# One core, one chain of attention, gated product and soft expert mixture: three moves in the schedule around the first block products

## The chip, the cores and the metric

The kernel runs as one program on one core of a Trainium2 chip. The core has five engines that run beside each other, each through its own list of instructions in order: TensorE (PE in the profile, with its weight loads as PEld), VectorE (DVE), ScalarE (ACT), GpSimd (POOL) and SyncE (SP, which here only issues DMAs). An engine that meets an instruction whose input is not there waits, and all that stands behind it in its list waits too. The metric is the device time of one execution in microseconds; lower is better.

## The reference, cut to what matters

```python
scores = scale * np.matmul(q, k.transpose(0, 1, 3, 2)) - np.log(S)   # 4 batches, 12 heads, S = 448, D = 64
attn = 1.0 / (1.0 + np.exp(-scores))
x = np.matmul(attn, v)            # then as (1792, 768)
x = (x @ w_a) * (x @ w_b) @ w_out # 768 -> 1536 -> 768
logits = x @ phi                  # 32 slots, softmax over tokens and over slots
d = softmax over tokens;  slot_input = d.T @ x
slot_out[e] = maximum(slot_input[e] @ w1[e], 0) @ w2[e]   # 8 experts, 4 slots each
return softmax over slots(logits) @ slot_out
```

## The kernel before

Attention runs in 24 pairs of heads, six for each of the four batches. A pair g needs its K and Q turned and split in two parts whose sum is the float32 value: `split_heads` writes kh, kl, qh and ql. From pair 13 on the turning is done by DVE (`transposed`, line 205), so that a pair costs DVE six instructions, in this order: transpose of K (kn), cast to kh (line 197), subtraction kl (line 198), transpose of Q (qn; a few pairs keep their Q in the tiles gk or hp, and rows name those), cast to qh, subtraction ql. In the dense stretch TensorE then does the scores of a pair in three chunks of two heads and three products each (line 260; the first chunk goes to a bank ms, and its third product is the one that reads ql), the part of the scores that two pairs share (line 275), and the product with V (line 294, and line 301 for the shared part). The sigmoids (line 266) are ACT's. ACT also copies a little of K (kr, line 228) for line 275. The result of a pair is copied from its bank by ACT or, for odd pairs, by DVE (line 323). These results, twelve tiles for batches 1 and 2, are the operands of what follows.

The products x @ w_a and x @ w_b of batches 1 and 2 are done together as one 2 by 2 block product in seven block products (Strassen's scheme with Winograd's additions), in twelve units of weight blocks; `unit` holds TensorE's side (line 874). Each of the seven has an operand made of x (A11, S2, A12, S3, S1, A22, S4) and one made of the weights. All are split in a high and a low part.

- `operands` makes the first three operands of x: casts on ACT or DVE, subtractions on POOL. For i in 0, 1, 2 it makes s2 by three subtractions on POOL (lines 800 to 802), and three steps later the cast S2h on DVE (line 782), the low part S2l on POOL (line 783), and a12 - s2 on POOL (line 806), which S4 needs later.
- `load_u(0)` has SP load 768 KB of weights (w_a and w_b as two fields) to the tile hp, line 737. `prep_u(0)` makes the second operands of the first unit from them: a cast on DVE (`block`, line 754) and a subtraction on POOL (line 755) for each of seven blocks, and four subtractions on POOL (lines 768 and 770) between the first block and the others. For all later units the cast is ACT's and the four subtractions are DVE's.

The order of all this is that of the program: a loop takes one step of attention (`att_g`), then one step of `operands`, and, in steps in which `operands` answers 0 or 1, one step of `prep_u`. SP issues DMAs in the same order; the loads of K, Q and V for pair g + 3 stand between those for the first unit. "Pair 16" and so on below are the values of g; results exist (`in xt`) as soon as their copy has been written down.

Behind the block products come the products of batch 3, done whole, and then the experts, whose weights (50 MB) are loaded in the order in which places for them come free, and the output tiles.

Of the kernel before, what the change touches and what calls it, by code (L numbers as in the profile page):

```python
# [14 lines left out]
ALU = mybir.AluOpType  # L15
# [12 lines left out]
NP = H // 2  # L28
# [3 lines left out]
GQ = 2 * NP + 2  # L32
# [9 lines left out]
def body(ctx, tc, q, k, v, w_a, w_b, w_out, phi, w1, w2, out):  # L42
    nc = tc.nc
    pe, act, dve, pool, sp = nc.tensor, nc.scalar, nc.vector, nc.gpsimd, nc.sync
# [11 lines left out]
    pools, r_all, hps_t = {}, [], []  # L56
# [27 lines left out]
    def gk_tile(i, dt=F32):  # L84
        return lgp.tile([128, 2048], dt, tag=f"lgp{i}", name=f"gk_{i}")

    gk_01 = [gk_tile(i) for i in range(2)]
# [216 lines left out]
    xt = {}  # L304
# [108 lines left out]
    late = []  # L413
# [175 lines left out]
    def fill_step():  # L589
        while fill:  # L590
            if next(fill[0], 0) is None:
                return
            fill.pop(0)
# [69 lines left out]
    def reload_gk(b, gi, t):  # L663
        if b in TURNED:
            sp.dma_start(out=t[:T], in_=gk32[b][gi].rearrange("t n f -> (t n f)").rearrange("(p x) -> p x", p=T))
            gtok[b, gi] = t.rearrange("p (c n) -> p c n", c=C)
            return
        t = t.rearrange("p (c n) -> p c n", c=C)
        src = gk32[b][gi].rearrange("n t f -> (n t) f")
        sp.dma_start(out=t[:, :3], in_=src[:384].rearrange("(c p) n -> p c n", c=3))  # L670
        sp.dma_start(out=t[64:, 3], in_=src[384:])
        gtok[b, gi] = t
# [59 lines left out]
    def load_u(u):  # L732
        if u > NU + 1:
            return
        t = hps_t[u % 2][:, :1536]
        src = ab32[u // 2 * 2:u // 2 * 2 + 2, u % 2] if u < NU else ab32[u - NU]
        sp.dma_start(out=t.rearrange("p (n c) -> p n c", n=2), in_=src.rearrange("n p c -> p n c"))
        if u < NU:
            wu[u] = t
        else:  # L740
            for i in range(2):
                w_raw[LAST + 2 * (u - NU) + i] = t[:, i * 768:(i + 1) * 768]
# [15 lines left out]
    def prep_u(u):  # L758

        w = wu.pop(u)  # L760
        b11, b21, b12, b22 = (w[:, i * BLK:(i + 1) * BLK] for i in range(4))
        t2, t3, t4 = (pools["cp"].tile([128, BLK], F32, tag=nm, name=nm) for nm in ("T2", "T3", "T4"))
        block(u, 0, b11)
        eng = dve if u else pool
        for o, a, b in ((t3, b22, b12), (b12, b12, b11), (t2, b22, b12)):
            if not u:
                yield
            eng.tensor_tensor(o, a, b, op=ALU.subtract)
        if not u:
            eng.tensor_tensor(t4, b21, t2, op=ALU.subtract)  # L770
            for _ in range(8):
                yield
        yield
        for m, t in ((1, t2), (2, b21), (3, t3), (4, b12), (5, t4), (6, b22)):
            if u and m == 5:
                eng.tensor_tensor(t4, b21, t2, op=ALU.subtract)  # L776
            block(u, m, t)
            yield

    def split_x(nm, i, t, pl, names, rnd=None, sub=None):  # L780
        xh, xl = (pl.tile([128, S], F32R, tag=x, name=x) for x in names)
        (rnd or dve.tensor_copy)(xh, t)
        (sub or pool).tensor_tensor(xl, t, xh.bitcast(F32), op=ALU.subtract)
        xs[nm, i] = xh, xl

    def operands():

        cp = pools["cp"]
        for i in range(3):
            split_x("A11", i, xt[NP + i], cp, (f"A11h{i}", f"A11l{i}"), act.copy)  # L790
            yield
            split_x("A12", i, xt[NP + 3 + i], cp, (f"A12h{i}", f"A12l{i}"), act.copy)
            yield
        for i in range(3):
            while 2 * NP + 3 + i not in xt:
                yield 1
            yield
            a11, a12, a21, a22 = (xt[n + i] for n in (NP, NP + 3, 2 * NP, 2 * NP + 3))
            s2 = cp.tile([128, S], F32, tag="s2", name="s2", bufs=2)
            pool.tensor_tensor(a11, a11, a21, op=ALU.subtract)  # L800
            pool.tensor_tensor(a21, a21, a22, op=ALU.add)
            pool.tensor_tensor(s2, a22, a11, op=ALU.subtract)
            for _ in range(3):
                yield
            split_x("S2", i, s2, cp, (f"S2h{i}", f"S2l{i}"))
            pool.tensor_tensor(a12, a12, s2, op=ALU.subtract)
            yield

    def late_operands(nm):
        n = {"S3": NP, "S1": 2 * NP, "A22": 2 * NP + 3, "S4": NP + 3}[nm]  # L810
# [388 lines left out]
    for kk in range(NP):  # L1199
# [6 lines left out]
    pools["cp"] = cp_ctx.enter_context(tc.tile_pool(name="cp", bufs=1, side="left"))  # L1206
    run["lsd2"] = (hps_t[0][:, 1536:1536 + S], hps_t[1][:, 1536:1536 + S], hps_t[2][:, 4 * S:4 * S + 128], hps_t[2][:, 4 * S + 128:])
    ops, pu = operands(), None
    then = [(2 * NP + 1, lambda: load_u(0)), (GQ + 5, lambda: reload_gk(0, 1, gk_01[1])),
            (GQ + 6, lambda: load_u(1)), (GQ + 7, lambda: reload_gk(0, 0, gk_01[0])),  # L1210
            (GQ + 7, lambda: reload_gk(0, 2, gk_2))]
    for cost in att_g:
        if then and then[0][0] in xt:
            then.pop(0)[1]()
        if not run.pop("trans", False):
            fill_step()
        run.pop("done", None)
        if next(ops, 0) in ((0, 1) if GQ + 1 in xt else (0,)):
            pu = pu or prep_u(0)
            next(pu, None)  # L1220
        if (4 * NP - 1, 0, C - 1) in a_t:
            break
# [97 lines left out]
    for n in range(0, len(order1), 4):  # L1320
        _, g, x, _ = order1[n]
# [7 lines left out]
        for j in range(4):  # L1329
            if order1[n + j] == order1[-1]:  # L1330
                _, pl, nm = ring.pop(order1[-1])
# [113 lines left out]
```

## Time and profile before

| | |
|---|---|
| median of three runs | 658.71 us (655.99, 658.71, 660.24) |
| the profiled execution's own time | 657.27 us |
| its span from the first to the last instruction | 655.5 us |
| TensorE, share of the span with a matmul in it | 96% |
| VectorE, ScalarE, GpSimd | 58%, 46%, 47% |
| attention in pairs 15 to 23, where the change lies | about 219 to 275 us |
| block products in twelve units | about 275 to 440 us |

Shares of the whole span say little here: the change lies in some 50 us of it, and there the engines' shares are others. Times in the rows below are microseconds from the first instruction. In the rows of the timeline the idle time in front of an instruction, and what ended it, stands at the end in brackets.

### The profile page before, as it was taken

Reading aid. Unit: us, or ns where it says so; the run is one execution under the profiler, and the core shown is the slowest. Engines: PE = TensorE matmul, PEld = TensorE weight load, DVE = VectorE, ACT = ScalarE, POOL = GpSimd, SP = SyncE. Lnnn points to the kernel's source line nnn. Section 1 sums busy time; section 2 is a strip of 40 time slices with the busy share of each in tenths; the row PEclk is TensorE's granted clock in tenths of the full one; section 3 lists DMA queues with packets and bytes.
Section 4 is the critical chain, followed back from the end, with each engine's and each line's share of the span. In section 5 each row is a group of like instructions: output and inputs, shape, how many; then the busy total and the mean of one; then the engine's idle time right before and its main releaser. Section 6 shows DMA issues by size and latency. Waiting matters only on the chain.

```text
span 655.5 us, 10847 instructions
## 1 busy us (share of the span) xinstructions
PE 627.6 (96%) x3989; PEld 448.3 (68%) x3989; DVE 379.5 (58%) x556; ACT 298.7 (46%) x540; POOL 309.5 (47%) x235
## 2 busy tenths in 40 slices
PE   8999999999999999999999999999999999996685
PEld 5556777777776554489988989897889895441121
DVE  4764877889793779488777766856233323030013
ACT  4988889889875877754422322201010002110012
POOL 0234587677772267369985576543335441000000
PEclk9999999999999999999999999999999999999788
DMA  9999889799778786901314332299899999999998
GB/s 222 265 284 259 262 281 342 248 298 298 255 178 209 138 165 118 287 2 48 97 50 104 91 109 75 81 241 307 239 359 405 414 340 366 419 399 416 409 369 298
DMA packets 148564, 159.76 MB, mean 244 GB/s; under 512 B 73584, under 2 KB 126640, under 8 KB 144432
## 3 DMA queue, kind: packets, MB, share of 16 engines
q1 hardware_dynamic: 145984, 157.35, 77.2%
q10 hardware_dynamic: 2528, 1.72, 0.8%
q8 instruction: 32, 0.52, 0.3%
q14 instruction: 20, 0.16, 0.1%
HBM read 129.11 MB, written 29.93 MB: 243 GB/s over the span
## 4 chain that ended last, share of the span: by engine, by line
PE 73%; DMA 14%; ACT 6%; DVE 3%; SPq 1%; issue 1%; POOL 1%; ACTq 0%; POOLq 0%; DVEq 0%
PE ab L686 22%; PE sc L874 16%; PE ab L874 8%; PE sc L260 6%; PE sc L288 4%; DMA misc<-clog 3%; PE ab L294 3%; DMA eb<-in_moe_w 2%; DMA e<-in_moe_w 2%; DMA hp<-in_moe_w 2%; ACT a L266 2%; DMA ea<-in_moe_w 1%; PE ms L600 1%; DMA ab<-w 1%; PE ms L213 1%
## 5 line engine op out<-in xcount | busy, mean ns | idle before, releaser
L472 POOL TENSOR_TENSOR w<-gk,cy 128x768 int32<-128x768 int32 x36 | 66.3, 1842 | 71.2 <-DVE gk L460 38.7
L266 ACT ACTIVATE a<-sc,sums 112x448 f32<-112x448 f32 (+1 forms) x149 | 84.0, 649 | 12.7 <-PE sc L260 12.7
L686 PE MATMUL ab<-t,wh 128*128 128x448 f32 x288 | 64.6, 370 | 0.0
L693 ACT COPY misc<-ab 128x448 f32<-128x448 f32 x24 | 12.7, 527 | 100.2 <-PE ab L686 100.2
L686 PEld LDWEIGHTS ab<-t,wh 128*128 128x128 f32 x288 | 53.7, 188 | 6.3 <-issue 1.3
L570 POOL TENSOR_TENSOR wl<-w,wh 128x768 fp32r<-128x768 f32 x24 | 46.1, 1923 | 11.5 <-ACT wh L569 11.5
L570 POOL TENSOR_TENSOR wl<-hp,wh 128x768 fp32r<-128x768 f32 x16 | 29.4, 1839 | 39.9 <-DVE wh L569 21.7
L288 PE MATMUL sc<-a,vn 112*64 112x448 f32 x192 | 38.7, 545 | 0.2 <-ACT a L266 0.2
L458 DVE TENSOR_SCALAR mf<-gk 128x768 f32<-128x768 f32 x24 | 22.7, 944 | 24.2 <-ACT gk L441 24.2
L696 DVE TENSOR_TENSOR misc<-misc,ab 128x448 f32<-128x448 f32 x24 | 14.7, 611 | 36.0 <-PE ab L686 36.0
L686 PE MATMUL ab<-xh,wl 128*128 128x448 f32 x144 | 34.8, 377 | 0.0
L754 ACT CAST wx<-T 128x384 fp32r<-128x384 f32 x19 | 9.7, 512 | 54.5 <-DVE T L776 36.7
L686 PE MATMUL ab<-xh,wh 128*128 128x448 f32 x144 | 34.5, 375 | 0.0
L686 PE MATMUL ab<-t,wl 128*128 128x448 f32 x144 | 34.3, 373 | 0.0
L686 PE MATMUL ab<-xl,wh 128*128 128x448 f32 x144 | 34.0, 372 | 0.0
L1404 DVE COPY o<-sc 128x384 f32<-128x384 f32 x10 | 5.4, 553 | 48.9 <-PE sc L1382 47.8
L755 POOL TENSOR_TENSOR wx<-hp,wx 128x384 fp32r<-128x384 f32 x27 | 31.5, 1171 | 4.6 <-DVE wx L754 2.5
L260 PE MATMUL sc<-qh,kh 64*112 64x448 f32 (+1 forms) x139 | 32.2, 432 | 1.0 <-ACT qh L197 0.6
L686 PEld LDWEIGHTS ab<-xh,wh 128*128 128x128 f32 x144 | 26.0, 188 | 7.3 <-issue 4.8
L686 PEld LDWEIGHTS ab<-xl,wh 128*128 128x128 f32 x144 | 26.4, 188 | 5.5 <-issue 3.5
L686 PEld LDWEIGHTS ab<-t,wl 128*128 128x128 f32 x144 | 26.6, 188 | 5.2 <-issue 2.0
L686 PEld LDWEIGHTS ab<-xh,wl 128*128 128x128 f32 x144 | 25.7, 188 | 5.1 <-issue 1.7
(509 smaller groups left out, 1571.3 us busy)
## 6 DMA issues: line engine op xcount, KB each, us to landing
hp<-ab SPq DMA_DIRECT2D x14, 768.0 KB, 4.4
gk<-gk SPq DMA_DIRECT2D x44, 224.0 KB, 4.3
ab<-w SPq DMA_DIRECT2D x24, 384.0 KB, 6.8
eb<-in_moe_w SPq DMA_DIRECT2D x7, 1024.0 KB, 12.8
ea<-in_moe_w SPq DMA_DIRECT2D x7, 1024.0 KB, 12.2
eb<-in_moe_w SPq DMA_DIRECT2D x7, 768.0 KB, 15.1
ea<-in_moe_w SPq DMA_DIRECT2D x7, 768.0 KB, 15.0
wr_cv<-in_moe_w_a SPq DMA_DIRECT2D x6, 768.0 KB, 8.0
```

The source lines that it names most:

```text
L260: pe.matmul(sc[h], kx[r, cs], qx[r], start=(i == 0), stop=(i == 2))
L266: act.activation(a, sc, AF.Sigmoid, bias=nlog[:n], scale=1.0 / math.sqrt(D))
L288: pe.matmul(pv[64 * h:64 * h + 64], qkv_t["v", g][:, h, c, :], a_t.pop((g, h, c)), start=(c == 0), stop=(c == C - 1))
L294: pe.matmul(pv[64 * h:64 * h + 64], qkv_t["v", g][:, h, c], a_t.pop((g, h, c)), start=(c == 0), stop=False)
L458: dve.tensor_scalar(mf, m, LOW, HIGH, op0=ALU.max, op1=ALU.min)
L472: pool.tensor_tensor(thirds(w), m.bitcast(I32), thirds(cy_t.pop(x)), op=ALU.add)
L570: pool.tensor_tensor(wl, t, wh.bitcast(F32), op=ALU.subtract)
L686: pe.matmul(t, w[:, kk * 128:(kk + 1) * 128], xt[b * NP + kk][xi], start=(s == 0 and kk == 0), stop=(s == 2 and kk == KD - 1))
L693: act.copy(gT_all[n % 5], t)
L696: dve.tensor_tensor(g, g, t, op=ALU.mult)
L755: pool.tensor_tensor(w[:, 1], t, w[:, 0].bitcast(F32), op=ALU.subtract)
L874: pe.matmul(t, w[:, wi, k * 128:(k + 1) * 128], xs[ORDER[m], k][xi], start=(s == 0 and k == 0), stop=(s == 2 and k == 2))
```

## The change

Three things change. (1) The cast S2h is written five steps behind its subtractions instead of three, and of the three subtractions a12 - s2 the second and the third are written behind all others. (2) `load_u(0)` is written when the result of pair 12 exists instead of pair 13's. (3) `prep_u(0)` may take steps from when pair 13's result exists, instead of pair 15's, in the steps in which `operands` waits for a result (it answers 1) as well as in those in which it has nothing left.

```diff
     def operands():
-        cp = pools["cp"]
+        cp, late = pools["cp"], []
...
-            for _ in range(3):
+            for _ in range(5):
                 yield
             split_x("S2", i, s2, cp, (f"S2h{i}", f"S2l{i}"))
+            if not i:
+                pool.tensor_tensor(a12, a12, s2, op=ALU.subtract)
+            else:
+                late.append((a12, s2))
+            yield
+        for a12, s2 in late:
             pool.tensor_tensor(a12, a12, s2, op=ALU.subtract)
-            yield
...
-    then = [(2 * NP + 1, lambda: load_u(0)), (GQ + 5, lambda: reload_gk(0, 1, gk_01[1])),
+    then = [(2 * NP, lambda: load_u(0)), (GQ + 5, lambda: reload_gk(0, 1, gk_01[1])),
...
-        if next(ops, 0) in ((0, 1) if GQ + 1 in xt else (0,)):
+        if next(ops, 0) in ((0, 1) if 2 * NP + 1 in xt else (0,)):
             pu = pu or prep_u(0)
             next(pu, None)
```

TensorE's and ScalarE's lists stay as they are. The list of SP around the weights' load (hp<-ab), before:

```order
L172 DMA vn<-in_v 128x2x192
L173 DMA vn<-in_v 64x2x64
L661 DMA gk_02_104<-gk_94 448x1x128 x4
L163 DMA kn<-in_k 32x14x32 x4
L163 DMA qn<-in_q 32x14x32 x4
L989 DMA clog_101<-hp_2474 448x1x32
L172 DMA gk_93<-in_v 128x2x192
L173 DMA gk_93<-in_v 64x2x64
L172 DMA gk_93<-in_v 128x2x192
L173 DMA gk_93<-in_v 64x2x64
L737 DMA hp_2472<-ab_99 128x2x768
L163 DMA kn<-in_k 32x14x32 x4
```

The same stretch of SP's list now:

```order
L172 DMA vn<-in_v 128x2x192
L173 DMA vn<-in_v 64x2x64
L737 DMA hp_2472<-ab_99 128x2x768
L661 DMA gk_02_104<-gk_94 448x1x128 x4
L163 DMA kn<-in_k 32x14x32 x4
L163 DMA qn<-in_q 32x14x32 x4
L994 DMA clog_101<-hp_2474 448x1x32
L172 DMA gk_93<-in_v 128x2x192
L173 DMA gk_93<-in_v 64x2x64
L172 DMA gk_93<-in_v 128x2x192
L173 DMA gk_93<-in_v 64x2x64
L163 DMA kn<-in_k 32x14x32 x4
```

The load has moved in front of 17 DMAs: four stores of gk, the K and Q of pair 18, one of clog and four for V. It now stands behind them no more, and the K of pair 19 follows V directly.

DVE's list, as one piece of the difference: the first two rows are the end of pair 15, the last three the beginning of pair 16, and between them stands the first cast of a block of weights, which before stood behind pair 18.

```order
 L197 CAST qh<-qn 128x448
 L198 TENSOR_TENSOR ql<-qn,qh 128x448
+L754 CAST wl_2698<-hp_2472 128x384
 L205 STREAM_TRANSPOSE kn<-kn 128x448
 L197 CAST kh<-kn 128x448
```

The next three casts of blocks move on the same list from behind pair 22 to behind pair 19 and the last three from behind pair 23 to behind pair 22. The cast S2h of i = 2, before in front of the copy of pair 19's result, is now behind it.

POOL's list from the last subtraction of A12 on, before:

```order
L783 TENSOR_TENSOR A12l_2594<-t_2398,A12h_2593 128x448
L800 TENSOR_TENSOR t_964<-t_964,hp_2474 128x448
L801 TENSOR_TENSOR hp_2474<-hp_2474,misc 128x448
L802 TENSOR_TENSOR s_2857<-misc,t_964 128x448
L783 TENSOR_TENSOR S2l_2909<-s_2857,S2h_2908 128x448
L806 TENSOR_TENSOR t_1791<-t_1791,s_2857 128x448
L755 TENSOR_TENSOR wl_2923<-hp_2472,wl_2923 128x384
L768 TENSOR_TENSOR T_2921<-hp_2472 128x384
L768 TENSOR_TENSOR hp_2472<-hp_2472 128x384
L768 TENSOR_TENSOR T_2920<-hp_2472 128x384
L770 TENSOR_TENSOR T_2922<-hp_2472,T_2920 128x384
```

POOL's list from there on now:

```order
L783 TENSOR_TENSOR A12l_2595<-t_2398,A12h_2594 128x448
L755 TENSOR_TENSOR wl_2698<-hp_2472,wl_2698 128x384
L768 TENSOR_TENSOR T_2696<-hp_2472 128x384
L768 TENSOR_TENSOR hp_2472<-hp_2472 128x384
L768 TENSOR_TENSOR T_2695<-hp_2472 128x384
L770 TENSOR_TENSOR T_2697<-hp_2472,T_2695 128x384
L800 TENSOR_TENSOR t_964<-t_964,hp_2474 128x448
L801 TENSOR_TENSOR hp_2474<-hp_2474,misc 128x448
L802 TENSOR_TENSOR s_2867<-misc,t_964 128x448
L783 TENSOR_TENSOR S2l_2938<-s_2867,S2h_2937 128x448
L807 TENSOR_TENSOR t_1791<-t_1791,s_2867 128x448
```

The five subtractions for the weights have changed places with the five for i = 0 of s2. Behind them come three more for the weights, then four for i = 1 and four for i = 2, then the two late ones and the last three for the weights.

## Rows read from the trace of the kernel before

**Rows 1.** The page's first part, busy time: engine, us (share), instructions.

```profile
PE 627.6 (96%) x3989; PEld 448.3 (68%) x3989; DVE 379.5 (58%) x556; ACT 298.7 (46%) x540; POOL 309.5 (47%) x235
```

**Rows 2.** Timeline of TensorE, 200 to 285 us: start, length, instruction, idle before it.

```profile
225.86 0.37 PE L260 MATMUL ms<-ql,kh 64*128 64x448 f32 x2
...
229.80 0.98 PE L301 MATMUL ab<-a,vn 64*64 64x448 f32 x8
...
232.82 2.48 PE L294 MATMUL ab<-a,gk 128*64 128x448 f32 x12
...
238.49 2.48 PE L294 MATMUL ab<-a,gk 128*64 128x448 f32 x12
...
244.42 2.48 PE L294 MATMUL ab<-a,vn 128*64 128x448 f32 x12
...
249.01 0.54 PE L260 MATMUL ms<-qh,kh 64*128 64x448 f32 x2 [0.62 <-DVE qh L197]
...
250.95 2.48 PE L294 MATMUL ab<-a,vn 128*64 128x448 f32 x12
...
256.38 2.48 PE L294 MATMUL ab<-a,gk 128*64 128x448 f32 x12
...
261.32 0.54 PE L260 MATMUL ms<-qh,kh 64*128 64x448 f32 x2 [0.97 <-DVE qh L197]
...
263.26 2.48 PE L294 MATMUL ab<-a,gk 128*64 128x448 f32 x12
265.91 1.50 PE L301 MATMUL ab<-a,gk 64*64 64x448 f32 x8 [0.17 <-ACT a L266]
```

**Rows 3.** Timeline of VectorE, pairs 16 and 19, a cast S2h, a cast of weights.

```profile
219.74 0.64 DVE L205 STREAM_TRANSPOSE kn<-kn 128x448 f32<-128x448 f32 x1
221.16 0.39 DVE L197 CAST kh<-kn 128x448 fp32r<-128x448 f32 x1 [0.78 <-PE sc L260]
...
223.23 0.62 DVE L198 TENSOR_TENSOR ql<-gk,qh 128x448 fp32r<-128x448 f32 x1
...
238.15 0.65 DVE L205 STREAM_TRANSPOSE kn<-kn 128x448 f32<-128x448 f32 x1 [1.38 <-DMA kn<-in_k]
238.90 1.19 DVE L197 CAST kh<-kn 128x448 fp32r<-128x448 f32 x1
...
242.58 1.32 DVE L198 TENSOR_TENSOR ql<-hp,qh 128x448 fp32r<-128x448 f32 x1
...
256.56 0.39 DVE L782 CAST S2h<-s 128x448 fp32r<-128x448 f32 x1 [1.06 <-POOL s L802]
...
262.02 0.35 DVE L754 CAST wl<-hp 128x384 fp32r<-128x384 f32 x1
262.29 1.16 DVE L754 CAST wx<-T 128x384 fp32r<-128x384 f32 x1
```

**Rows 4.** Timeline of GpSimd, the wait for pair 15's result and the weights' subtractions.

```profile
231.67 1.15 POOL L801 TENSOR_TENSOR hp<-hp,misc 128x448 f32<-128x448 f32 x1 [14.40 <-DVE misc L323]
...
238.84 1.00 POOL L755 TENSOR_TENSOR wl<-hp,wl 128x384 fp32r<-128x384 f32 x1
...
243.50 1.27 POOL L770 TENSOR_TENSOR T<-hp,T 128x384 f32<-128x384 f32 x1
```

**Rows 5.** Timeline of SyncE's DMA issues, 200 to 232 us.

```profile
217.97 0.65 SPq L173 DMA_DIRECT2D vn<-in_v  x1
...
231.17 0.59 SPq L737 DMA_DIRECT2D hp<-ab  x1
```

**Rows 6.** DMA issues at 231, at 263 and in 285 to 330 us: count, size, us to landing.

```profile
hp<-ab SPq DMA_DIRECT2D x1, 768.0 KB, 5.2
...
hp<-ab SPq DMA_DIRECT2D x1, 768.0 KB, 7.7
...
hp<-ab SPq DMA_DIRECT2D x3, 768.0 KB, 4.3
```

**Rows 7.** Busy time in stretches of the tail: PE, PEld, DVE, ACT, POOL, granted clock, DMA.

```profile
590.00:600.00 10.00, 5.94 (x50) 1.59 (x42) 0.00 (x0) 0.00 (x0) 0.00 (x0) 1.00 1.02 416
600.00:605.00 5.00, 3.61 (x30) 1.06 (x30) 0.00 (x0) 0.00 (x0) 0.00 (x0) 1.00 1.02 417
605.00:610.00 5.00, 3.52 (x18) 0.93 (x22) 0.00 (x0) 0.00 (x0) 0.00 (x0) 0.61 1.02 419
```

## The prediction

> **What bounds the kernel now.** I read the page's busy times first: TensorE has a matmul in 96% of the span [rows 1], so the most that any schedule can give is a few per cent, and the change can only touch what TensorE loses in the 50 us where instructions move. Next the timeline of TensorE there, for gaps and for rhythm. Gaps: 0.62 us at 249.0 and 0.97 us at 261.3, both ended by VectorE's qh, and 0.17 us at 265.9, ended by a sigmoid [rows 2]. Rhythm: the products with V begin at 232.82, 238.49, 244.42, 250.95, 256.38 and 263.26 [rows 2]. Undisturbed steps are 5.67 us (to 238.49, a step with the shared scores) and 5.43 us (250.95 to 256.38); the others are 5.93, 6.53 and 6.88, that is 0.50, 0.86 and 1.21 us too long. So 2.57 us are lost there, and with the 0.17 us about 2.7. That is all that a better order of VectorE's and GpSimd's work can win.
>
> Why VectorE is late is in its own timeline. Pair 16 has GpSimd idle beside it: from the start of its kn (219.74) to the end of ql (223.23 + 0.62 = 223.85) are 4.11 us, less a wait of 0.78, so 3.33 us of work; its cast kh takes 0.39 [rows 3]. Pair 19 has the block's subtraction and the four others beside it (238.84 to 243.50 + 1.27) [rows 4]: from 238.15 to the end of ql (242.58 + 1.32 = 243.90) are 5.75 us, with the cast kh at 1.19 and ql at 1.32 instead of 0.62 [rows 3]. So 4.4 GpSimd instructions cost VectorE 2.4 us, 0.55 each. A pair of TensorE lasts 5.5 us, so VectorE keeps up while GpSimd rests and falls behind while it works; and GpSimd rests 14.4 us in front of 231.67 [rows 4], where VectorE has room.
>
> The Trainium skill, "SBUF — State Buffer", section "Who interferes with whom", says why: casts in the fast mode and subtractions of two SBUF operands need a port that VectorE and GpSimd take in turn, each for a whole instruction. Taken strictly (four such instructions in a pair, each held back by a whole GpSimd instruction of about 1.15 us), pair 16 would take 3.33 + 4.6 = 7.9 us and the first stall below would be 2.2 us longer; the trace has 5.75 us for that case, so the sum goes by the trace.
>
> **The change part by part.** *The load goes sooner.* SP's issues follow each other closely, so the load is issued when the V load in front of it is out: 217.97 + 0.65 = 218.6, instead of 231.17 [rows 5]. A load of this size landed 5.2 us after issue at 231, 7.7 at 263 behind other large transfers, 4.3 in the quiet stretch [rows 6]. So it lands at 222.9 to 226.3; I take 5.2, the nearest in place and traffic, so 223.8. The loads that it delays by its own issue (0.6 us) are for pair 18, far ahead of their use. And it no longer stands in front of pair 19's K: VectorE's wait of 1.38 us for that at 238.15 [rows 3] should go.
>
> *The first cast goes sooner, too soon.* VectorE reaches it behind pair 15, when pair 16's kn starts now, at 219.74 [rows 3]. The data come at 223.8. VectorE waits about 4.1 us, and behind it in its list stand all six instructions of pair 16. TensorE needs the last of them, ql, at 225.86 [rows 2] and has it at 223.85, so 2.0 us of the wait are covered. After it come the cast, 0.35 alone [rows 3], and pair 16, now with GpSimd's five subtractions beside it as pair 19 has them today: 223.8 + 0.35 + 5.75 = 229.9. TensorE would be 4.0 us late there. Bounds: landing at 222.9 and 3.33 us for an undisturbed pair give 226.6, 0.7 us late; landing at 226.3 and 5.75 give 232.4, 6.5 us late. I take 4.0, since both its inputs are the nearest rows.
>
> *What comes back.* (a) Pair 17 on VectorE has one or two GpSimd instructions beside it, 3.33 + 0.8, and ends at 234.0; the copy of pair 15's result waits for line 301, which ends at 229.80 + 0.98 + 4.0 = 234.8 [rows 2]. So from here VectorE and TensorE are both 4.0 us behind the old trace. (b) In front of pair 19 VectorE loses neither the 1.38 us for K nor the first cast (0.35): 2.3 behind. Pair 19 has two GpSimd instructions beside it (S2l, and the first a12 - s2) instead of 4.4: 1.3 less, so 1.0 behind at its end. (c) Now three casts of weights stand here, 0.27 between the starts of two of them and 1.16 for the one beside GpSimd [rows 3], 1.7 together: 2.7 behind; their three subtractions put about one more GpSimd instruction beside pair 20: 3.2 behind at its ql. TensorE, 4.0 behind less the 0.50 it no longer waits in the step to 244.42, needs pair 20's ql 0.62 sooner than it came before: 2.9 behind is the latest without a wait. It waits 0.3 and is 3.2 behind. (d) The cast S2h waited 1.06 us for GpSimd at 256.56 [rows 3]; two steps later it doesn't: 2.1 behind; the two late subtractions run in pair 22: 2.7 behind at its ql, and TensorE with it, having lost less at 261.3 than before. (e) The three casts behind pair 22 are still three casts in the same place, so pair 23's kn, ACT's kr behind it and the sigmoid that TensorE waits for at 265.91 [rows 2] come 2.7 late as well. The last three casts no longer stand behind pair 23, which nobody waited for.
>
> So of 4.0 us lost at pair 16 some 1.3 are regained: +2.7. Since VectorE's lateness at (c) and (d) rests on 0.55 us per GpSimd instruction and each step could be out by half of that, I take +2. From 275 us on TensorE's list and its order are the same, and the block products run without gaps, so the shift is handed on to the end whole, the expert loads included, which begin when TensorE frees their places.
>
> **The sum.** The profiled execution took 657.27 us, 1.4 below the median of the three others; 657.3 + 2 = 659.3 against its own time, 660.7 against the median. The four executions have their centre at 658.0; I take 658.0 + 2 = 660.0.
>
> **Rivals.** *Nothing is lost at pair 16 and the late stalls go* (faster). It needs the load to land by 223 and VectorE to pass GpSimd's five subtractions nearly undisturbed: then the stall is 0.7 us, and the 2.7 us lost later come back because GpSimd's work has moved to where VectorE had room: -2.0, 656. For it: the load does land in 4.3 us in a quiet stretch [rows 6], and TensorE's gaps all hang on VectorE. Against it: pair 19 shows what five subtractions do to a pair, and three casts still stand in front of pair 23.
>
> *The stall is larger and stays* (slower). One mechanism: the first cast at the head of VectorE's list waits for a transfer that shares the DMA engines with the four stores of gk issued right behind it. With 7.7 us to landing TensorE stands at pair 16 for 6.5 us; it decides from a landing of about 6 us on. With the same 1.3 us regained: +5.2, 663.2. For it: the load at 263 took 7.7 [rows 6]. Against: there the large transfer stood in front of it, here behind.
>
> *The clock falls.* In the tail, stretches with TensorE 59% and 72% busy at a granted clock of 1.00 are followed by one at 0.61 [rows 7], so part of that was at the lower of its two levels, 1.2 GHz. A single stall of 2 to 4 us is longer than any wait of TensorE in this stretch now (0.97). If the clock fell for the 5 us of such a row at 0.61, TensorE would lose about 2 us more: +4, 662. The Trainium skill, "TensorE: Matmul & The Clock Gate", section "Part 1: The HAM clock gate", states that an idle engine falls to 1.2 GHz and gets 2.4 GHz back by working; the trace agrees that there are these two levels, and no row of this stretch shows a fall.
>
> *The moves do nothing.* The first cast's wait is covered and VectorE is late as before: 0, 658. It would need the pair's slack of 2.0 us to be 4.
>
> **Chances.** Forecast (a stall at pair 16, partly regained, +0.5 to +3.5): 0.50. Late stalls gone (-2.7 to -0.5): 0.20. Nothing: 0.10. Stall that stays: 0.12. Clock: 0.08. For 8 in 10 the range takes the forecast, the nothing and most of the faster and slower cases, with the 2 us by which single medians stray: 656.0 to 664.0. Within 1% (6.6 us) is what a measurement of this kernel can't tell from no change; the faster case never reaches it, and the slower ones only at their upper ends: faster 0.02, same 0.92, slower 0.06.
>
> **What the new profile would show.** The cast of the first block idle some 4 us until a DMA, at 223 to 226; TensorE's first-chunk scores of pair 16 waiting 2 us or more for qh or ql; GpSimd's five subtractions at 224 to 230 instead of 239 to 245; no wait for pair 19's K; no wait of S2h for GpSimd; TensorE's gaps near 250 and 262 smaller; the block products beginning 1 to 3 us later. The prediction is wrong if the cast doesn't wait, or if pair 16 takes VectorE under 4 us with the subtractions beside it, or if pairs 20 to 23 run at 5.5 us a step throughout, so that all is regained.

## The result, and the profile after

The changed kernel takes 661.82 us (median of 14 runs, 658.9 to 664.88) where the kernel before takes 658.58 us beside it on the same chips (14 runs, 655.71 to 661.19). The ratio is 1.0055 with an interval of 1.0038 to 1.0073, that is 2.5 to 4.8 us longer: within 1%, and yet clear of no change, since the interval does not touch 1. The profiled execution took 660.3 us, its span is 658.4 us.

The page of the kernel after has busy time, share of the span and number of instructions of each engine:

```profile
PE 628.4 (95%) x3989; PEld 448.5 (68%) x3989; DVE 383.0 (58%) x556; ACT 298.9 (45%) x540; POOL 309.9 (47%) x235
```

The same work as in [rows 1], so the place has to be looked for in the stretch in which instructions moved. VectorE there, answering to [rows 3]:

```profile
219.51 0.63 DVE L198 TENSOR_TENSOR ql<-qn,qh 128x448 fp32r<-128x448 f32 x1
223.37 0.36 DVE L754 CAST wl<-hp 128x384 fp32r<-128x384 f32 x1 [3.23 <-DMA hp<-ab]
223.64 0.64 DVE L205 STREAM_TRANSPOSE kn<-kn 128x448 f32<-128x448 f32 x1
...
227.01 0.52 DVE L197 CAST qh<-gk 128x448 fp32r<-128x448 f32 x1
227.56 1.31 DVE L198 TENSOR_TENSOR ql<-gk,qh 128x448 fp32r<-128x448 f32 x1
...
240.32 0.64 DVE L205 STREAM_TRANSPOSE kn<-kn 128x448 f32<-128x448 f32 x1
...
259.37 0.38 DVE L782 CAST S2h<-s 128x448 fp32r<-128x448 f32 x1
```

The first cast waits 3.23 us for the load, and with it all of pair 16 behind it: kn starts at 223.64 instead of 219.74. Pair 16 then takes from 223.64 to 227.56 + 1.31 = 228.87, 5.23 us. Pair 19's kn (240.32) and the cast S2h (259.37) have no bracket any more: these two waits are gone. The load on SP's queue (answering to [rows 5]) and GpSimd (to [rows 4]):

```profile
218.29 0.54 SPq L737 DMA_DIRECT2D hp<-ab  x1
```

```profile
223.81 1.01 POOL L755 TENSOR_TENSOR wl<-hp,wl 128x384 fp32r<-128x384 f32 x1 [7.20 <-DVE wl L754]
...
228.47 1.27 POOL L770 TENSOR_TENSOR T<-hp,T 128x384 f32<-128x384 f32 x1
```

The load is issued 13 us sooner and its cast begins 5.1 us after the issue; the five subtractions, 223.81 to 229.74, lie beside pair 16. TensorE, answering to [rows 2]:

```profile
222.08 2.48 PE L294 MATMUL ab<-a,vn 128*64 128x448 f32 x12
...
227.68 0.71 PE L260 MATMUL ms<-qh,kh 64*128 64x448 f32 x2 [1.62 <-DVE qh L197]
228.15 0.61 PE L260 MATMUL ms<-qh,kl 64*128 64x448 f32 x2
228.93 0.74 PE L260 MATMUL ms<-ql,kh 64*128 64x448 f32 x2 [0.17 <-DVE ql L198]
229.60 1.77 PE L275 MATMUL sc<-qn,kr 64*64 64x448 f32 x8
231.30 2.48 PE L294 MATMUL ab<-a,vn 128*64 128x448 f32 x12
236.73 2.48 PE L294 MATMUL ab<-a,gk 128*64 128x448 f32 x12
242.48 2.48 PE L294 MATMUL ab<-a,gk 128*64 128x448 f32 x12
247.91 2.48 PE L294 MATMUL ab<-a,vn 128*64 128x448 f32 x12
253.00 0.54 PE L260 MATMUL ms<-ql,kh 64*128 64x448 f32 x2 [0.66 <-DVE ql L198]
254.38 2.48 PE L294 MATMUL ab<-a,vn 128*64 128x448 f32 x12
259.81 2.48 PE L294 MATMUL ab<-a,gk 128*64 128x448 f32 x12
264.11 0.54 PE L260 MATMUL ms<-qh,kh 64*128 64x448 f32 x2 [0.34 <-DVE qh L197]
266.06 2.48 PE L294 MATMUL ab<-a,gk 128*64 128x448 f32 x12
```

For pair 16 the kernel before had, in the same place:

```profile
221.64 2.48 PE L294 MATMUL ab<-a,vn 128*64 128x448 f32 x12
...
225.45 0.37 PE L260 MATMUL ms<-qh,kh 64*128 64x448 f32 x2
...
226.16 1.31 PE L275 MATMUL sc<-qn,kr 64*64 64x448 f32 x8
227.40 2.48 PE L294 MATMUL ab<-a,vn 128*64 128x448 f32 x12
```

A new gap of 1.62 us stands at pair 16; those at 249.0 and 261.3 of [rows 2] are now 0.66 at 253.0 and 0.34 at 264.1. Behind the new gap the products are longer: 0.71 and 0.74 us where before they were 0.37, and 1.77 for the shared scores where before they were 1.31. The granted clock by stretch says why (time of the stretch; busy time and count of PE, PEld, DVE, ACT, POOL; clock, DMA share, GB/s):

```profile
222.00:226.00 4.00, 4.00 (x26) 2.02 (x24) 2.50 (x4) 2.91 (x7) 2.13 (x2) 1.00 0.97 282
226.00:227.70 1.70, 0.08 (x4) 0.06 (x2) 1.63 (x4) 1.70 (x4) 1.61 (x2) 1.00 0.71 120
227.70:231.30 3.60, 3.43 (x14) 1.04 (x14) 3.46 (x4) 1.45 (x4) 3.20 (x3) 0.53 0.67 126
231.30:236.00 4.70, 4.70 (x36) 2.36 (x34) 2.91 (x6) 2.02 (x4) 0.42 (x1) 1.00 0.64 129
```

TensorE, busy for 0.08 us of the 1.70 before, works the next 3.6 us mostly at the lower of its two levels (0.53, that is 1.2 GHz), and then at full speed again.

**Where the time went.** I count the steps between the first products with V of one pair and the next (L294), nine of them from about 222 us on; the last ends just behind the first of the block products. Before they add up to 55.06 us, after to 57.41, +2.35. The step that holds pair 16's scores is 9.22 instead of 5.76: +3.46. The other eight add up to 48.19 instead of 49.30: −1.11, of it 0.50 in the step to 247.91 (5.43 for 5.93), 0.06 in that to 254.38 and 0.63 in that to 266.06, while the one to 242.48 is 0.08 longer. Another 0.44 us were there before the stretch (222.08 for 221.64). The first block product begins at 277.46 instead of 274.67, 2.79 later, and the span ends 2.9 later: hardly anything is given back or lost behind 277 us.

### The profile page after: what moved, and what is told of

It reads as the page before. It is cut to its first block, busy times and chain, and to the rows that moved or that the text cites. A ratio compares the mean times of both kernels' runs of the same rounds, so it can differ in the third digit from the quotient of the medians.

```text
span 658.4 us, 10844 instructions
## 1 busy us (share of the span) xinstructions
PE 628.4 (95%) x3989; PEld 448.5 (68%) x3989; DVE 383.0 (58%) x556; ACT 298.9 (45%) x540; POOL 309.9 (47%) x235
## 4 chain that ended last, share of the span: by engine, by line
PE 71%; DMA 14%; ACT 5%; DVE 4%; issue 2%; SPq 1%; ACTq 0%; POOL 0%; DVEq 0%; POOLq 0%
PE ab L686 23%; PE sc L879 16%; PE ab L879 8%; PE sc L260 5%; PE sc L288 4%; DMA misc<-clog 3%; DMA e<-in_moe_w 3%; ACT a L266 2%; DMA eb<-in_moe_w 2%; DMA hp<-in_moe_w 2%; PE ab L294 2%; DMA gk<-gk 1%; DMA ea<-in_moe_w 1%; PE ms L213 1%; DMA ab<-w 1%
```

## The experiments

All twelve in one table. "Pair 16" is that one step less 5.76 us, "later" the sum of the eight others less 49.30 us, both of one trace each; the last column is the ratio of the timed runs to the kernel before, with its interval.

| run | differs | pair 16 | later | ratio |
|---|---|---|---|---|
| after | | +3.46 | −1.11 | 1.0055 [1.0038, 1.0073] |
| e1_load_back | after, load where it was | +16.84 | −0.62 | 1.0266 [1.0236, 1.0297] |
| e2_load_sooner | after, load sooner still | +0.19 | −1.10 | 1.0002 [0.9987, 1.0017] |
| e3_cast_behind_16 | after, casts from behind pair 16 on | 0.00 | −0.45 | 1.0012 [0.9991, 1.0034] |
| e4_gate_back | after without part 3 | 0.00 | −1.49 | 0.9984 [0.9967, 1.0001] |
| e5_s2_back | after without part 1 | +5.40 | +3.62 | 1.0099 [1.0065, 1.0133] |
| e6_s2_alone | before with part 1 alone | 0.00 | −1.45 | 0.9983 [0.9967, 0.9999] |
| e7_load_alone | before with part 2 alone | −0.01 | −0.11 | 1.0021 [1.0000, 1.0042] |
| e8_sooner_spread | e2, casts spread out | +0.13 | −1.56 | 0.9996 [0.9978, 1.0015] |
| e9_subs_later | after, weights' subtractions later | +1.59 | −1.54 | 1.0009 [0.9986, 1.0031] |
| e10_sooner_spread_late | e8, late S2 subtractions | +0.14 | −2.21 | 0.9986 [0.9971, 1.0001] |
| e11_gate_back_late | e4, late S2 subtractions | −0.01 | −0.73 | 0.9984 [0.9965, 1.0003] |
| e12_behind_16_spread_late | e3, spread, late S2 subtractions | 0.00 | −1.12 | 1.0001 [0.9981, 1.0021] |

The theory: the loss is the first cast's wait for the load, plus the five subtractions beside pair 16. The rivals: the S2 part makes the loss, or the wait is harmless and the loss comes from elsewhere.

**e1_load_back: more of the suspected wait.**

```diff
-    then = [(2 * NP, lambda: load_u(0)), ...
+    then = [(2 * NP + 1, lambda: load_u(0)), ...
```

> The changed kernel with the load of the first unit's weights back in its old place in SyncE's list, all else as changed. Theory (VectorE's list is blocked by the first cast, which waits for the load): the load goes out at about 231 us and lands at about 236.4 instead of 223.4, so VectorE waits some 16 us in front of pair 16 and TensorE stands 13 us longer there than in the changed kernel; of that about 1 us is regained later: 12 to 15 us slower than before. Rival 1 (the loss comes from GpSimd's five subtractions beside pair 16 and from the casts in front of pair 20, not from the wait): 2 to 4 us slower, as the changed kernel. Rival 2 (the loss comes from the later S2 casts): 2 to 4 us slower.

Measured: 675.11 us beside 658.59. VectorE, TensorE and a window of this run:

```profile
236.10 0.36 DVE L754 CAST wl<-hp 128x384 fp32r<-128x384 f32 x1 [16.65 <-DMA hp<-ab]
```

```profile
240.38 0.74 PE L260 MATMUL ms<-qh,kh 64*128 64x448 f32 x2 [15.01 <-DVE qh L197]
```

```profile
240.00:244.00 4.00, 3.49 (x14) 1.12 (x14) 3.83 (x5) 1.85 (x4) 3.54 (x3) 0.50 0.63 103
```

The load starts 13 us later, the cast waits 13.4 us longer, TensorE's gap grows by 13.4 and the step by 13.4. The wait at the head of VectorE's list is paid nearly one for one, and the scores behind it again ran at the lower clock (0.50). By the timed runs it is 17.5 us slower than before, somewhat more than the 12 to 15 expected.

**e2_load_sooner: less of it.**

```diff
-    then = [(2 * NP, lambda: load_u(0)), ...
+    then = [(2 * NP - 1, lambda: load_u(0)), ...
```

> The changed kernel with the load written when pair 11's result exists, one pair of heads sooner still; the lists of all other engines stay. Theory: the load goes out at about 213 us, lands by 219, and the first cast doesn't wait; TensorE waits at most 0.5 us at pair 16, from the subtractions beside it; the time is that of before less 0.5 to 1.5 us (the later gaps were 1.1 us smaller in the changed kernel). Rival 1 (GpSimd's subtractions and moved casts make the loss): still 2 to 4 us slower than before. Rival 2 (S2): still 2 to 4 us slower.

Measured: 658.2 us, no different from before, where a gain of 0.5 to 1.5 us was expected. The load is issued at 214.94; VectorE:

```profile
221.76 0.35 DVE L754 CAST wl<-hp 128x384 fp32r<-128x384 f32 x1
222.03 0.64 DVE L205 STREAM_TRANSPOSE kn<-kn 128x448 f32<-128x448 f32 x1
...
226.93 1.32 DVE L198 TENSOR_TENSOR ql<-gk,qh 128x448 fp32r<-128x448 f32 x1
```

No bracket at the cast. Pair 16 still has the subtractions beside it (ql 1.32), but with no wait ahead of it TensorE's step is only 0.19 too long. So the subtractions alone are nearly covered by VectorE's lead; it is the wait that uses the lead up.

**e3_cast_behind_16 and e4_gate_back: the wait taken away by a later first cast.**

```diff
-        if next(ops, 0) in ((0, 1) if 2 * NP + 1 in xt else (0,)):
+        if next(ops, 0) in ((0, 1) if GQ + 2 in stk else (0,)):   # e3
+        if next(ops, 0) in ((0, 1) if GQ + 1 in xt else (0,)):    # e4
```

> The changed kernel with the load as changed, but the weights' casts and subtractions held until pair 16's split has been written, so that the first cast stands behind pair 16. Theory: VectorE reaches the cast at about 224.3 us, after the landing at 223.4, and TensorE has no wait at pair 16; five casts now stand in front of pair 23 and cost up to 1 us there; 0 to 1.5 us faster than before. Rival 1: the subtractions now stand beside pair 17, so the loss moves there, 1 to 4 us slower. Rival 2: 2 to 4 us slower.

> The changed kernel with the old gate for putting the weights together (pair 15's result): the load sooner and the S2 casts later are kept, the first cast stands behind pair 18 as before, the other six behind pair 23. Theory: nothing waits for the load and pair 19's K comes without its 1.38 us wait; VectorE carries no cast between pairs 19 and 23: 0.5 to 2.5 us faster than before. Rival 1: also faster, so this run doesn't tell them apart. Rival 2: 2 to 4 us slower.

Measured: 659.9 us (e3) and 657.46 (e4). In both the step of pair 16 is 5.76 again, and e4 gains what was expected of it, though its interval just reaches no change. e3 gains nothing. It pays elsewhere, since its casts stand five in a row in front of pair 23, and the sigmoid behind it is late:

```profile
267.16 1.50 PE L301 MATMUL ab<-a,gk 64*64 64x448 f32 x8 [1.86 <-ACT a L266]
```

The length of that pair's step goes with the number of casts of weights that stand in front of pair 23 in VectorE's list: 6.45 us with none (e4, e6, e8, e9, e10, e12), 7.20 to 7.22 with three (before, after, e1, e2, e7), 7.47 with four (e11), 8.90 with five (e3). Only e5, with none and 6.72, falls out. And behind e3's gap, a longer one than that of after, the clock did not fall:

```profile
267.16:270.00 2.84, 2.84 (x22) 1.80 (x24) 2.35 (x5) 1.37 (x3) 0.87 (x1) 1.00 0.93 300
```

e4 keeps the sooner load and the S2 part and has one gap of 0.71 us left:

```profile
260.45 0.54 PE L260 MATMUL ms<-qh,kh 64*128 64x448 f32 x2 [0.71 <-ACT a L266]
```

Of the three parts it is the third, the sooner first cast, that loses where the load is not there in time; without it the change is 0.1 us slower to 2.2 us faster than before by the interval.

**e5_s2_back: does the S2 part make the loss?**

```diff
-            for _ in range(5):
+            for _ in range(3):
...
-            if not i:
-                pool.tensor_tensor(a12, a12, s2, op=ALU.subtract)
-            else:
-                late.append((a12, s2))
+            pool.tensor_tensor(a12, a12, s2, op=ALU.subtract)
```

> The changed kernel with the S2 part undone (the casts S2h three steps behind their subtractions, each a12 - s2 right behind them), load and gate as changed. The first cast stands in front of pair 16 as in the changed kernel. Theory (the cast's wait for the load): VectorE waits about 3 us there and TensorE loses 3 to 4 us at pair 16; with the casts spread otherwise behind it, 2 to 4 us slower than before. Rival (the S2 part makes the loss): within 1 us of before.

Measured: 666.11 us beside 657.97, worse than the theory's figure and opposite to the rival's. VectorE, TensorE and a window:

```profile
225.54 0.36 DVE L754 CAST wl<-hp 128x384 fp32r<-128x384 f32 x1 [5.22 <-DMA hp<-ab]
```

```profile
229.82 0.74 PE L260 MATMUL ms<-qh,kh 64*128 64x448 f32 x2 [3.57 <-DVE qh L197]
```

```profile
229.80:236.00 6.20, 6.05 (x22) 2.12 (x24) 5.24 (x7) 2.66 (x6) 3.24 (x3) 0.50 0.66 133
```

Two things are worse here. The cast waits 2.0 us longer than in the trace of after, since in this execution the load was issued 0.9 us later (219.18) and took 6.4 us from there; that gives the 5.40 at pair 16, with the lower clock from 229.8 to 236 behind it. And the later steps add up to 52.92 us, 4.7 more than after's 48.19, with gaps of 0.98, 0.64 and 1.71 us at 256.5, 257.9 and 270.3. Of the 4.7 us, 1.47 lie in the step right behind pair 16 (6.90 for 5.43), which has no gap in it and begins at the lower clock, and behind the last gap the clock fell again:

```profile
270.30:272.00 1.70, 1.66 (x10) 1.07 (x14) 1.56 (x4) 0.52 (x3) 0.00 (x0) 0.58 0.28 108
```

So the S2 part does not make the loss. What it gives back in the later steps this run doesn't show by itself: the stall ahead, the clock and the places of the casts of weights (two now in front of pair 19, one in front of pair 22, none in front of 23) differ from after as well.

**e6_s2_alone and e7_load_alone: the two parts by themselves, on the kernel before.** The edits are the change's own hunks in `operands`, and its one line in `then`.

> The kernel before with the S2 part of the change alone: load and gate as before. Six casts now stand behind pair 23 instead of three, since the steps that take them come later. Theory: no wait at pair 16; pair 19's K still waits about 1.4 us behind the weights' load; the gaps near 262 us go since no cast stands in front of pair 23: 0 to 1.5 us faster than before. Rival (the S2 part makes the loss): 2 to 4 us slower.

> The kernel before with the load alone written one pair sooner; the lists of VectorE, GpSimd, TensorE and ScalarE are those of before. Theory: the load has landed long before its first cast (behind pair 18), and pair 19's K no longer waits behind it, so VectorE gains 1.4 us in front of pair 19 and TensorE's gap near 249 us (0.86 us of its step) goes; the gap near 262 us stays: 0.5 to 1.5 us faster than before. Rival (the wait for K was covered): no change.

Measured: 657.17 us (e6) and 659.12 (e7). e6 regains 1.45 us in the later steps, and its interval ends at 0.9999. Of the 1.45 us, 0.77 lie in the step of pair 23, since without the sooner gate the later S2 steps push three casts of weights from in front of pair 23 to behind it, a thing that the whole change does not do; 0.60 lie in the step of pair 22, as in after. e7 does what the prediction's part on the load says, as pair 19's kn (237.77) shows no wait:

```profile
237.50 0.35 DVE L754 CAST wl<-hp 128x384 fp32r<-128x384 f32 x1
237.77 0.64 DVE L205 STREAM_TRANSPOSE kn<-kn 128x448 f32<-128x448 f32 x1
```

But it gains nothing, a miss of my expectation: the gap of [rows 2] near 249 is gone, and in its place the one near 262 is larger and ended by a sigmoid, so that 1.28 us gained at pairs 19 and 20 are lost again, all but 0.2, at pairs 21 and 22:

```profile
262.26 0.54 PE L260 MATMUL ms<-qh,kh 64*128 64x448 f32 x2 [1.31 <-ACT a L266]
```

**e8_sooner_spread: e2 with the casts spread out.**

```diff
-            for _ in range(8):
+            for _ in range(4):
```

> A version meant to beat both: the changed kernel with the load one pair sooner still (as in the run before with the load sooner), and the pause between the four subtractions and the second block cut from eight steps to four, so that three casts stand behind pair 17, where VectorE waits 1.7 to 2.5 us for TensorE anyway, one behind pair 18, two behind pair 19, and none in front of pairs 20 to 23. Theory: no wait at pair 16 and only the sigmoid's gap of 0.2 us near 266 left, less than 1 us lost in the stretch instead of 2.6: 1 to 2.5 us faster than before. Rival (GpSimd's subtractions set VectorE's lateness wherever they stand): within 0.7 us of before.

Measured: 658.15 us, the same as before, another miss. The later steps gain 1.56 us by the trace; the timed runs show −1.4 to +1.0.

**e9_subs_later: the subtractions apart from the wait.** The first cast stays where the change puts it, but the first block's low part and the four subtractions behind it stand on GpSimd's list behind S2's of i = 0. The other six casts come behind pair 23 by it, so what the timed runs show is not the subtractions' price alone; the step of pair 16 is what counts.

```diff
-        pool.tensor_tensor(w[:, 1], t, w[:, 0].bitcast(F32), op=ALU.subtract)
+        low = lambda: pool.tensor_tensor(w[:, 1], t, w[:, 0].bitcast(F32), op=ALU.subtract)
+        if (u, m) == (0, 0):
+            run["low0"] = low
+        else:
+            low()
...
+        if not u:
+            while "s2" not in run:
+                yield
+            run.pop("low0")()
...
             pool.tensor_tensor(s2, a22, a11, op=ALU.subtract)
+            run["s2"] = True
```

> The changed kernel with the first cast where the change has it, in front of pair 16, but with GpSimd's five subtractions for the weights behind those of s2 for i = 0, as before, so that GpSimd rests beside pair 16. The other six casts come behind pair 23, so that this differs from the run with the old gate in the place of that one cast. Theory (a wait of 3 to 4 us for the load, and on top of it 1.5 to 2.4 us of GpSimd beside pair 16): VectorE still waits 3 to 4 us for the load, but pair 16 takes it 3.3 us, and TensorE loses 1 to 2 us at pair 16 instead of 3.5; within 1 us of before. Rival (the wait alone makes the 3.5 us): TensorE loses 3 us or more at pair 16; 1.5 to 3 us slower than before.

Measured: 658.47 us beside 658.18. VectorE, TensorE and two windows:

```profile
225.27 0.36 DVE L754 CAST wl<-hp 128x384 fp32r<-128x384 f32 x1 [3.96 <-DMA hp<-ab]
225.55 0.64 DVE L205 STREAM_TRANSPOSE kn<-kn 128x448 f32<-128x448 f32 x1
...
228.36 0.63 DVE L198 TENSOR_TENSOR ql<-gk,qh 128x448 fp32r<-128x448 f32 x1
```

```profile
228.47 0.54 PE L260 MATMUL ms<-qh,kh 64*128 64x448 f32 x2 [1.38 <-DVE qh L197]
```

```profile
227.00:228.50 1.50, 0.12 (x4) 0.06 (x2) 1.43 (x4) 1.50 (x4) 0.00 (x0) 1.00 0.78 148
228.50:232.00 3.50, 3.50 (x22) 1.53 (x24) 3.30 (x7) 3.43 (x8) 0.00 (x0) 1.00 0.65 103
```

The cast waits longer than in after (3.96 for 3.23 us), and yet the step is only 1.59 us too long instead of 3.46. With GpSimd at rest (0.00 in both windows) pair 16 takes 225.55 to 228.99, 3.44 us instead of 5.23, and behind the gap of 1.38 us the clock stayed at 1.00. So the wait alone does not make the whole loss; the subtractions and the lower clock have their part. This run takes both away together, and as e3 keeps its clock behind a gap of 1.86 us, it doesn't show that the clock held because the subtractions were gone. What tells the two apart is the trace of after.

**e10 to e12: is there a better version?** e8, e4 and e3 again, with the S2 subtractions of i = 1 and 2 held back until the K and Q of pairs GQ + 7 and 4 NP − 1 are made; e12 also spreads the casts (`range(2)`). The edit is e12's; e10 and e11 write the same condition at greater length.

```diff
-            while 2 * NP + 3 + i not in xt:
+            while 2 * NP + 3 + i not in xt or (i and (0, GQ + 7, 4 * NP - 1)[i] not in stk):
```

> The version with the load sooner and the casts spread, and in addition the s2 part for i = 1 and 2 written behind pairs 21 and 23: S2l of i = 1 then waits on GpSimd for its cast behind pair 22, and nothing of GpSimd's runs beside pairs 21 and most of 22; the last six subtractions run behind pair 23's, where VectorE and TensorE need nothing of them. Theory (GpSimd beside VectorE costs 0.55 us an instruction and makes the gaps near 250 and 262 us): the gap at pair 22 goes, the one at pair 20 stays in part, 1.5 to 3 us faster than before. Rival (the gaps come from the casts' places alone): as the version with the casts spread, within 0.7 us of before.

> The run with the old gate and the load one pair sooner, with the same two parts of s2 written behind pairs 21 and 23. Five of the six casts then stand on either side of pair 23. Theory: GpSimd works beside pairs 19 and 20 as in the run with the old gate, not beside 21 and 22; four casts in front of pair 23 cost 1 us there; 1 to 2 us faster than before. Rival: as the run with the old gate or slower by those casts, 0.5 us faster than before at most.

> A version meant to beat both: the load where the change puts it, the first cast held until pair 16 is written (as in that run), the pause between the four subtractions and the second block cut from eight steps to two, so that two casts stand behind pair 17, one behind 18 and three behind 19 and none in front of pairs 21 to 23, and the s2 part for i = 1 and 2 written behind pairs 21 and 23. Theory: no wait at pair 16, one gap left at pair 20 (0.7 to 1.1 us of its step), none at 22 and 23; the stretch loses 1 us instead of the 2.6 of before: 1 to 2.5 us faster than before. Rival (the time saved in the stretch doesn't reach the end): within 0.5 us of before.

Measured: 657.38 us (0.9986), 657.51 (0.9984) and 659.18 (1.0001). By the ratios that is 0.9, 1.1 and 0.0 us, where at least 1.5, 1 and 1 were expected: e10 and e12 are misses, and e11 is not told from no change. e12's step of pair 20 is 7.58 us long, where before it was 6.53. In e10 one gap is left in the whole stretch:

```profile
251.24 0.53 PE L260 MATMUL ms<-ql,kh 64*128 64x448 f32 x2 [0.66 <-DVE ql L198]
```

It is the shortest stretch of all, 2.07 us under before by its trace, while the timed runs show 0.9 us, with an interval that touches no change. e6 stays the only version whose interval lies under 1, by a hair, and among twelve versions that can be chance.

## Why the prediction was right, and where its sizes were off

**The load.** Forecast: issue 218.6, landing 5.2 later, 223.8. Measured: 218.29, and the cast at 223.37, 5.1 later. In the eight traces with the load in this place the cast, or the landing where nothing waits, came 5.1 to 6.4 us after the issue (after 5.1, e7 5.3, e9 and e12 5.4, e4 5.5, e11 5.6, e3 5.8, e5 6.4), so what the prediction took lies at the lower end of what occurs; its bounds went to 7.7.

**The first cast.** Forecast: a wait of 4.1 us in front of pair 16, then 5.75 us for the pair, TensorE 4.0 late. The mechanism was right: e1 makes the wait 13.4 us longer and TensorE loses 13.4 us more; e2, e3 and e4 take it away and the step is 5.76 to 5.95. Its sizes were 3.23, 5.23 and 3.46. The last splits into 1.79 us by which the first product with qh is late against the rhythm, 0.84 more at the first with ql, and 0.83 from there to the products with V, at the lower clock. So VectorE made TensorE 2.63 us late and not 4.0, and that the whole comes so near the forecast is in part luck: the clock, which the forecast left out, added the 0.83. The price of a GpSimd instruction beside VectorE is smaller than the 0.55 us assumed: 5.23 − 3.44 = 1.79 us between after and e9, for the 4.3 of them that lie inside pair 16, 0.4 each; in e1 and e5 the pair took 5.19 and 5.20 us. The prediction's count of 4.4 beside pair 19 was short: the end of a subtraction of line 806 (237.74 to 238.88) lay there too, and with it the same rows give 0.5. The Trainium skill, "SBUF — State Buffer", section "Who interferes with whom", has the two engines hold a port in turn; these rows agree that there is a price in a pair's casts and subtractions. The prediction's strict working of it, 7.9 us for the pair, is not what happened: the two casts and two subtractions were each held back by 0.13 to 0.69 us (after against e9), not by a whole instruction of GpSimd.

**What comes back.** Forecast 1.3 of 4.0, measured 1.11 of 3.46. (b) K's wait at pair 19 is gone, and the 0.50 us in the step to 247.91 are regained as forecast. (c) TensorE waits 0.66 us at pair 20, not 0.3, so that step regains 0.06 and not 0.3. (d) S2h doesn't wait, and the step to 266.06 regains 0.63. (e) the step to 273.26 is 7.20 for 7.22, as late as before. The runs of single parts say which part pays: the 0.63 is the S2 part's, since e6 has 6.28 in that step and e7, the load alone, 7.22 (before 6.88); the 0.50 comes with either (5.46 and 5.43, before 5.93).

**What there was to win.** The prediction counted 2.7 us, with 0.17 of them, the gap, at pair 23. But that step is 7.22 us in before and 6.45 in the six traces without the casts in front of pair 23, so 0.77 us are lost there, and about 3.3 in all. The change keeps three casts in that place and could not win this part; e10, which moves them away, has the shortest stretch.

**The clock.** The mechanism of the rival with a chance of 0.08 came beside the forecast's, in a smaller size: 0.83 us in the trace, not 2. The fall lasted 3.6 us, and in the first 1.25 of them (227.68 to 228.93) TensorE had VectorE's ql to wait for anyway. In e9, at the full clock, the products from the first with ql to those with V take 1.43 us; in after they take 2.37. In e1 and e5 the clock was at 0.50 for 4.0 us and more. Whether it fell in the other executions of the changed kernel its one trace doesn't say. The Trainium skill, "TensorE: Matmul & The Clock Gate", section "Part 1: The HAM clock gate", states that idleness brings the lower clock and work the higher; after, e1 and e5 agree, while in e3 and e9 the clock stays at 1.00 behind gaps of 1.86 and 1.38 us.

**The sum.** The step that was mis-sized is the last one, where the working gave +2.7 and I took +2 for the regained part's uncertainty. The trace has +2.35 in the stretch and +2.9 in the span, the timed runs +3.6 by the ratio (2.5 to 4.8) and 3.2 by the medians. The rounding went to the wrong side, and a stall adds its clock, which the sum left out. With that the time, 661.8, came to lie in the upper half of 656 to 664. And 6.6 us is not the least that this measurement can tell from no change, as the prediction has it: 14 executions of each kernel gave an interval 2.3 us wide.

**The signs.** None of the three signs of being wrong was seen. Of the others, two did not come as said: TensorE's wait at pair 16 was 1.62 us for qh and 0.17 for ql, not 2 or more, and the gap near 250 did not shrink (0.66 for 0.62).

**What stays open.** Most kernels here come out about 1 us slower by the timed runs than the nine steps of their one trace say against the one trace of before (e2 −0.91 and +0.1, e8 −1.43 and −0.3, e10 −2.07 and −0.9, e12 −1.12 and +0.1; e4, e6 and e9 by half of that or less, e5 and e11 not). Either that one execution of before took longer in this stretch than most do, or something of a microsecond is lost elsewhere; the runs don't tell. The spans of the single traces can't settle it either, since what lies on either side of the stretch scatters by more: in the fourteen traces it begins at 221.4 to 223.8 us (before 221.6), and from the first block product to the end are 379.8 to 382.4 us (before 380.8).

## What to carry to other kernels

Before the first use of a load is moved forward in an engine's list, add the load's issue and a slow landing, not the quiet one, and compare it with when the engine reaches that place: what stands behind it in the list, here all of one pair's inputs, waits too. GpSimd's work beside VectorE reaches TensorE only where VectorE has no lead (0.19 us in e2), so moving it into idle time pays when nothing else has just used that lead up. Read lost time from the rhythm of the steps and not from the gaps alone: pair 23 showed a gap of 0.17 us and lost 0.77. Of a change in three parts, time the parts apart: here one gained about a microsecond, hardly clear of noise, one nothing, and the third, beside the other two, took more than they gave.

## What the runs showed of the hardware

The same 768 KB load in the same place of the queue took 5.1 to 6.4 us from issue to landing or use in eight executions, a spread larger than what the change won in all later steps together (1.11). Behind a gap of TensorE of 1.62 us the granted clock was 0.53 for 3.6 us, behind 3.57 us (e5) 0.50 for at least 6.2 us, and behind 1.71 us (e5) 0.58 in the next 1.7 us; behind gaps of 1.38 (e9) and 1.86 us (e3) it was 1.00. So the length of the gap alone does not tell whether the clock falls. In the trace of after the fall added 0.83 us to a stall of 2.6 (1.79 + 0.84). And a GpSimd subtraction of 1.0 to 1.3 us beside VectorE's casts and subtractions cost those 0.4 us (after against e9).
